# Selective attention with a SwiGLU block: earlier k and q copies, weight differences in eight pieces, and a subtraction and two stores at the end on GpSimd

## The chip, the cores and the metric

The kernel runs on one core of a Trainium2 chip. A core has TensorE (PE: matmuls, with weight loads, PEld, beside them), VectorE (DVE), ScalarE (ACT), GpSimd (POOL) and SyncE (SP), which here only issues transfers. The metric is the device time of one execution in microseconds (us). The span, which the profile shows, is the time from the first to the last instruction; it is some 1.8 us shorter than the metric in the kernel before.

## The reference, cut to what matters

```python
def _attn_ref(q, k, v, s):                 # 8 batches, 8 heads, 576 positions, 64 wide
    scores = scale * np.matmul(q, k.transpose(0, 1, 3, 2))
    bias = -(cum[:, :, :, None] - cum[:, :, None, :])      # cum: running sum of max(s, 0)
    scores = np.where(causal, -1000000000.0, scores + np.minimum(bias, 0.0))
    ...                                    # softmax
    return np.matmul(attn, v)

def _moe_ref(x, w_gate, w_val, w_out):     # 4608 tokens, 512 wide, 1536 inside
    g = x @ w_gate
    silu = g * (1.0 / (1.0 + np.exp(-g)))
    return silu * (x @ w_val) @ w_out
```

The attention of all heads, laid side by side, is the block's input x.

## The kernel before

TensorE gets one stream of matmuls in which attention (64 heads in 16 groups of four) and the block's nine tiles of 512 tokens are interleaved. The parts that matter:

From group 5 on, k and q reach their place as transposes by DMA (tiles pk, pq); VectorE then copies them to where the score matmuls read them. The copies wait in a list, from which each item of the block takes one or none:

```python
def split(hb, name, r):
    nc.vector.tensor_copy(KQ[hb % 2][r][64 * r : 64 * r + 64, kq, 0 : NR * S],
                          prs[name, hb][64 * r : 64 * r + 64, :])
...
first = 2 if late else 1                     # late: group 5
if step in (first, first + 1) and ci == 1:   # step: the head within the group before
    for r in range(NR):
        later.append((split, hb, "kq"[step - first], r))
```

From the third tile on the last product is done with seven block products in place of eight, for which sums and differences of the output weights are needed. VectorE makes the four differences in the third tile, in place:

```python
W_DIFFS = [(j, i) for i in (3, 4) for j in range(2)]
...
if todo and (i >= 24 if tt < FIRST7 else i % 4 == 2):
    weight_op(*todo.pop(0))
```

In the very last tile (`end`), the first of two groups of 128 rows ends with a subtraction and two stores, on GpSimd in other tiles, on VectorE and SyncE here. The second group, `ending`, follows on VectorE with three stores on SyncE:

```python
(nc.vector if end else nc.gpsimd).tensor_sub(y[:, 0:4:3, :], y[:, 0:4:3, :], y[:, 1:3, :])
flush()
def store(eng=nc.sync if end else nc.gpsimd):
    for i in range(2):
        eng.dma_start(out[a + i * HT : a + i * HT + 128, :], y[:, 2 * i : 2 * i + 2, :]...)
```

The softmax here doesn't subtract the row's maximum and nothing guards it: scores larger than these inputs give would overflow.

Of the kernel before, what the change touches and what calls it, by code (L numbers as in the profile page):

```python
# [19 lines left out]
def kernel(  # L20
# [11 lines left out]
    nc = tc.nc  # L32
# [47 lines left out]
    NPE = 5  # L80
# [23 lines left out]
    first = first_sbuf.enter_context(tc.tile_pool(name="first", bufs=1))  # L104
# [4 lines left out]
    with tc.manual_schedule():  # L109
# [35 lines left out]
        def view(b, w):  # L145
            return bank[b][:, 0:w]
# [15 lines left out]
        def load_qk(hb):  # L162
            load_one(hb, "k")
            load_one(hb, "q")

        def load_v(b, cs):
            if 0 in cs:
                loaded["v", b] = raw.tile([128, NCH, H, D], FP32, tag="rawv", bufs=1, name="rawv")
            t = loaded["v", b]
            for c in cs:  # L170
                n = 128 if c < 4 else TAIL
                nc.sync.dma_start(
                    t[0:n, c, :, :],
                    v[b, :, c * 128 : c * 128 + n, :].rearrange("h p d -> p h d"),
                )

        def cast_v(b, c, eng):
            n = 128 if c < 4 else TAIL
            dst, src_t = VT[b % 2][0:n, c, :, 0:D], loaded["v", b][0:n, c, :, :]
            if eng is nc.scalar:  # L180
                nc.scalar.copy(dst, src_t)
            else:
                eng.tensor_copy(dst, src_t)
# [8 lines left out]
        def aug(hb, engs):  # L192
            for hh in range(HB):
                r, e = divmod(hh, 2)
                r0 = 64 * (1 - r)
                bh = hb * HB + hh
                engs[hh].dma_start(  # L197
                    KQ[hb % 2][r][r0 : r0 + 4, :, e * S : (e + 1) * S],
                    HL[bh : bh + 1, :, :, :],
                )  # L200
# [48 lines left out]
        def cast_one(hb, name, eng):  # L249
            cts[name, hb] = cp.tile([128, J, NR, D], BF16, tag="c" + name, bufs=2, name="c" + name)  # L250
            dst = cts[name, hb].rearrange("x j r d -> x r j d")
            src_t = loaded[name, hb]
            if eng is nc.scalar:
                nc.scalar.copy(dst, src_t)
            else:
                eng.tensor_copy(dst, src_t)
# [11 lines left out]
        def scratch(hb):  # L268
            for name, SC in (("k", KS), ("q", QS)):
                nc.sync.dma_start(  # L270
                    SC[hb].rearrange("(x j) c -> x (j c)", j=J),
                    cts[name, hb].rearrange("x j r d -> x (j r d)"),
                )
# [3 lines left out]
        def transposes(hb):  # L277
            for name, SC in (("k", KS), ("q", QS)):
                prs[name, hb] = cp.tile([128, NR * S], BF16, tag="p" + name, bufs=1, name="p" + name)
                nc.sync.dma_start_transpose(prs[name, hb], SC[hb])  # L280
# [194 lines left out]
        def do_later(n):  # L475
            while n > 0 and later:
                f, *args = later.pop(0)
                f(*args)
                n -= 1

        def side(h, step, ci):
            bh = HB * h + step
            if bh == H + 3 and ci == 1:
                for c in range(5):
                    cast_v(1, c, nc.gpsimd)
            if h >= 3 and h + 3 < NHB and (step, ci) == (0, 1):
                load_qk(h + 3)
            hb = h + 1
            if NPE <= hb < NHB:
                late = hb == NPE  # L490
                if (step, ci) == (0, 1):
                    if late:
                        transposes(hb)
                    aug(hb, GP4)
                first = 2 if late else 1
                if step in (first, first + 1) and ci == 1:
                    for r in range(NR):
                        later.append((split, hb, "kq"[step - first], r))
            hb = h + 2
            if NPE <= hb < NHB:  # L500
                late = hb == NPE
                if (step, ci) == ((1, 1) if late else (0, 2)):
                    cast_one(hb, "k", nc.scalar)
                if (step, ci) == ((2, 1) if late else (1, 2)):
                    cast_one(hb, "q", nc.scalar)
                if (step, ci) == ((3, 1) if late else (2, 0)):
                    scratch(hb)
                if (step, ci) == (3, 3 if hb == NPE + 1 else 0) and not late:
                    do_later(NR * 2)
                    transposes(hb)  # L510
            if ci != 1:
                return
            bn = h // 2 + 1
            if 2 <= bn < B:
                if h % 2 == 0:
                    if step == 2:
                        load_v(bn, (0, 1))
                    if step == 3:
                        load_v(bn, (2, 3, 4))
# [65 lines left out]
        FIRST7 = 2  # L585
# [9 lines left out]
        def wo_parts(j):  # L595
            w = WO[j].rearrange("p (a h) (d n) -> p a h d n", h=2, d=2)
            return w, WS[:, j * (WKO // 2) : (j + 1) * (WKO // 2), :, :]

        def weight_op(j, i):
            w, t = wo_parts(j)  # L600
            if i == 0:
                nc.vector.tensor_add(t[:, :, 0, :], w[:, :, 0, 0, :], w[:, :, 1, 1, :])
            elif i == 1:
                nc.vector.tensor_add(t[:, :, 1, :], w[:, :, 0, 0, :], w[:, :, 0, 1, :])
            elif i == 2:
                nc.vector.scalar_tensor_tensor(
                    t[:, :, 2, :], in0=w[:, :, 1, 0, :], scalar=-1.0,
                    in1=w[:, :, 1, 1, :], op0=ALU.mult, op1=ALU.subtract,
                )
            elif i == 3:  # L610
                nc.vector.tensor_sub(
                    w[:, :, 0, 1, :], w[:, :, 0, 1, :], w[:, :, 1, 1, :]
                )
            else:
                nc.vector.tensor_sub(
                    w[:, :, 1, 0, :], w[:, :, 1, 0, :], w[:, :, 0, 0, :]
                )
# [71 lines left out]
        def down_seven(tt, hps, sus):  # L689
            W = [wo_parts(p // (WKO // 2))[0][:, p % (WKO // 2)] for p in range(NP)]  # L690
            end = tt == NTT - 1
# [49 lines left out]
            def m7(g):  # L741
                product(half(g, "1", "6")[0], False, True,
                        lambda p: hps[p][:, 2, cols[g]], lambda p: WS[:, p, 2, :])
# [22 lines left out]
            def seventh(g):  # L766
                a = tt * TT + g * 128
                y = Y[g]
                m7(g)
                nc.vector.tensor_add(  # L770
                    y[:, 0:4:3, :], DE[g],
                    view(B[g]["1"], DM).rearrange("p (a n) -> p a n", a=2),
                )
                give_banks(g, "1", "6")
                (nc.vector if end else nc.gpsimd).tensor_sub(  # L775
                    y[:, 0:4:3, :], y[:, 0:4:3, :], y[:, 1:3, :]
                )
                flush()

                def store(eng=nc.sync if end else nc.gpsimd):  # L780
                    for i in range(2):
                        eng.dma_start(
                            out[a + i * HT : a + i * HT + 128, :],
                            y[:, 2 * i : 2 * i + 2, :].rearrange("p a n -> p (a n)"),
                        )

                stores.append(store)
                if end:
                    flush()
                yield 0.757  # L790
# [149 lines left out]
                    state["pos"] = 1e9  # L940

        W_SUMS = [(j, i) for i in range(3) for j in range(2)]
        W_DIFFS = [(j, i) for i in (3, 4) for j in range(2)]
        LAGS = [0, 1.65] + [3.6] * NTT
        hook = {
            1: [lambda: prep_one(2, 0)],
# [5 lines left out]
        for tt in range(NTT):  # L952
            lo = H * (tt + 1) + LAGS[tt]
            hi = min(H * (tt + 2) + LAGS[tt + 1], BH + 2)
            span = 36 if tt < FIRST7 else 34.5
            if hi == BH + 2:
                span = 30
            n0 = 6 if tt == 0 else 0
            n = 0
            todo = {FIRST7 - 1: W_SUMS, FIRST7: W_DIFFS}.get(tt, [])  # L960
            for i, cost in enumerate(ffn_items(tt)):
                n += cost
                if todo and (i >= 24 if tt < FIRST7 else i % 4 == 2):
                    weight_op(*todo.pop(0))
                if i >= 2 * NFT or i % 4 == 1:
                    do_later(1)
                for f in hook.pop(n, ()):
                    f()
                pump(lo + (hi - lo) * min(1.0, max(0, n - n0) / (span - n0)))
# [31 lines left out]
```

## Time and profile before

| | before |
|---|---|
| time, median of the first 3 executions | 383.06 us (382.67 to 383.71) |
| span of the profiled execution, clock | 381.3 us, 1.000 |
| TensorE busy | 363.5 us, 95% |
| VectorE busy | 289.6 us, 76% |
| start of the last weight load | 376.26 us |
| last landing of a store | 380.41 us |

TensorE is the bound, so the time is read from where its stream stops, and from what comes after its end. Its busy time alone does not tell that, as ends of matmuls are modelled; start-to-start times do. The lines behind this are shown in the prediction.

### The profile page before, as it was taken

What the parts mean: (1) busy time and instruction counts of PE and PEld (TensorE: products, weight loads), DVE (VectorE), ACT (ScalarE), POOL (GpSimd) and SP (SyncE); (2) the same over time, 40 slices, a digit from 0 to 9 for tenths busy, and PEclk for the clock granted to TensorE, in tenths of its full rate; (3) what the DMA queues carried; (4) which work ended last, traced back from release to release, by engine and by line L of the source; (5) the groups of instructions that cost most, each with busy time, mean ns of one, the idle gap of its engine ahead of it and who ended that gap; (6) DMA issues with size and microseconds to landing.
All of it is one profiled execution on the core that took longest, in us unless ns stands there. A gap on an engine that the chain in (4) does not pass through costs nothing. (4 is left out here: it accounts for less than half of the span.)

```text
span 381.3 us, 8674 instructions
## 1 busy us (share of the span) xinstructions
PE 363.5 (95%) x3246; PEld 230.5 (60%) x3246; DVE 289.6 (76%) x577; ACT 242.7 (64%) x459; POOL 205.9 (54%) x326
## 2 busy tenths in 40 slices
PE   3779999998999999999999999999999999999995
PEld 3666556655555555865586558655875575476464
DVE  8666787456895799868986899589958866975983
ACT  8586788676977786578767876697455523323321
POOL 6684357545364636595458647775665426315220
PEclk9999999999999999999999999999999999999999
DMA  7999999997477998498739965987223213002003
GB/s 234 197 253 263 198 242 268 348 259 162 163 167 246 236 285 220 105 287 216 194 114 285 270 149 158 252 179 166 37 80 101 32 19 127 0 2 97 14 2 110
DMA packets 100729, 64.22 MB, mean 168 GB/s; under 512 B 81888, under 2 KB 85824, under 8 KB 100688
## 3 DMA queue, kind: packets, MB, share of 16 engines
q1 hardware_dynamic: 91248, 46.15, 48.6%
q0 software_dynamic: 9440, 17.53, 17.7%
q8 instruction: 25, 0.41, 0.4%
q14 instruction: 16, 0.13, 0.1%
HBM read 37.90 MB, written 19.86 MB: 151 GB/s over the span
## 5 line engine op out<-in xcount | busy, mean ns | idle before, releaser
L388 ACT ACTIVATE pt<-bank 128x512 bf16<-128x512 f32 x224 | 106.7, 506 | 26.5 <-PE bank L375 18.3
L626 PE MATMUL bank<-XT,wg 128*128 128x512 bf16 x432 | 110.9, 379 | 0.6 <-DVE pp L633 0.2
L641 PE MATMUL bank<-XT,wv 128*128 128x512 bf16 x432 | 110.8, 379 | 0.2
L631 ACT ACTIVATE th<-bank 128x512 bf16<-128x512 f32 x108 | 64.7, 599 | 60.0 <-PE bank L626 54.7
L633 DVE SCALAR_TENSOR_TENSOR pp<-th,bank 128x512 bf16<-128x512 bf16 x108 | 73.9, 684 | 30.2 <-ACT th L631 29.5
L649 DVE SCALAR_TENSOR_TENSOR ht<-pp,bank 128x512 bf16<-128x512 bf16 x108 | 74.1, 686 | 10.3 <-POOL ht L658 0.5
L658 POOL TENSOR_TENSOR ht<-ht 128x512 bf16<-128x512 bf16 x35 | 40.4, 1154 | 53.9 <-DVE su L656 53.8
L375 PE MATMUL bank<-kq 128*128 128x128 bf16 (+4 forms) x504 | 67.5, 240 | 1.6 <-DVE kq L284 1.1
L375 PEld LDWEIGHTS <-kq 128*128 128x128 bf16 x576 | 46.7, 99 | 34.8 <-issue 5.7
L641 PEld LDWEIGHTS <-wv 128*128 128x128 bf16 x432 | 38.6, 98 | 35.8 <-issue 0.4
L626 PEld LDWEIGHTS <-wg 128*128 128x128 bf16 x432 | 38.5, 98 | 35.2 <-issue 1.2
L391 POOL TENSOR_SCALAR_AFFINE_SELECT pt<-pt 128x512 bf16<-128x512 bf16 x64 | 41.8, 653 | 28.5 <-ACT pt L388 28.1
L413 PEld LDWEIGHTS <-pt 128*128 128x128 bf16 x960 | 41.1, 98 | 16.0
L413 PE MATMUL bank<-vt,pt 128*128 128x65 bf16 x840 | 41.8, 194 | 0.0
L447 POOL DMA_DIRECT2D xs<-ot x24 | 21.9, 912 | 31.7 <-DVE ot L430 31.7
L711 PEld LDWEIGHTS <-ht 128*128 128x128 bf16 x336 | 31.2, 98 | 4.3
L197 POOL DMA_DIRECT2D kq<-HL x52 | 31.2, 602 | 0.1
L430 DVE TENSOR_TENSOR ot<-bank,rc 128x320 bf16<-128x320 f32 x56 | 27.5, 492 | 1.9
L396 POOL TENSOR_SCALAR_AFFINE_SELECT pt<-pt 128x64 bf16<-128x64 bf16 x64 | 16.7, 261 | 18.9 <-ACT pt L388 18.7
L711 PEld LDWEIGHTS <-su 128*128 128x128 bf16 x252 | 23.6, 98 | 3.3
L670 PE MATMUL bank<-wo,ht 128*128 128x512 bf16 x96 | 24.6, 379 | 0.0
L775 POOL TENSOR_TENSOR ysb<-ysb 128x512 f32<-128x512 f32 x12 | 15.2, 1271 | 15.3 <-DVE ysb L770 15.3
(96 smaller groups left out, 396.9 us busy)
## 6 DMA issues: line engine op xcount, KB each, us to landing
rawk<-in_k_dram SPq DMA_DIRECT2D x15, 576.0 KB
rawq<-in_q_dram SPq DMA_DIRECT2D x15, 576.0 KB
rawv<-in_v_dram SPq DMA_DIRECT2D x32, 256.0 KB
out_dram<-ysb POOLq DMA_DIRECT2D x32, 256.0 KB, 3.8
xs<-ot POOLq DMA_DIRECT2D x24, 160.0 KB, 3.7
ks<-ck SPq DMA_DIRECT2D x11, 288.0 KB
qs<-cq SPq DMA_DIRECT2D x11, 288.0 KB
wg<-in_moe_w_gate_dram POOLq DMA_DIRECT2D x2, 768.0 KB, 12.6
```

Source lines behind the costliest of these rows:

```text
L197: engs[hh].dma_start(KQ[hb % 2][r][r0 : r0 + 4, :, e * S : (e + 1) * S], HL[bh : bh + 1, :, :, :],)
L375: nc.tensor.matmul(sc[:, o : o + w], T[:, 1, e * S + 128 * tj : e * S + 128 * (tj + 1)], T[:, 0, e * S + lo : e * S + hi], start=True, sto ...
L388: nc.scalar.activation(pt[:, c0 : c0 + W], sc[:, 0:W], AF.Exp, scale=0.125)
L391: nc.gpsimd.affine_select(pt[:, 1088:1600], pt[:, 1088:1600], pattern=[[0, 4], [1, 128]], compare_op=ALU.is_ge, fill=zreg, base=0, channel ...
L413: nc.tensor.matmul(av[:, bi * (D + 1) : (bi + 1) * (D + 1)], pt[:, c0 : c0 + 128], VT[b % 2][:, tj, h, :], start=(tj == 0), stop=(tj == bi),)
L626: nc.tensor.matmul(pg, WG[j][:, c, f0 : f0 + 128], xt[:, c, :], start=(c == 0), stop=(c == 3),)
L631: nc.scalar.activation(th, pg, AF.Tanh, scale=0.5)
L633: nc.vector.scalar_tensor_tensor(pp, in0=th, scalar=1.0, in1=pg, op0=ALU.add, op1=ALU.mult)
L641: nc.tensor.matmul(pv, WV[j][:, c, f0 : f0 + 128], xt[:, c, :], start=(c == 0), stop=(c == 3),)
L649: nc.vector.scalar_tensor_tensor(hp[:, 2 * k2 : 2 * k2 + 2, :].rearrange("p a n -> p (a n)"), in0=pp, scalar=0.5, in1=pv, op0=ALU.mult, op ...
L658: (nc.vector if ft == NFT - 1 else nc.gpsimd).tensor_sub(hp[:, 1:3, :], hp[:, 1:4:2, :], hp[:, 0:3:2, :])
L711: nc.tensor.matmul(ps, lhs(p), rhs(p), start=(first and p == 0), stop=(last and p == NP - 1), skip_group_check=True,)
```

## The change

Its intent: copies listed one or two heads sooner should be done before TensorE asks for them; differences in pieces of two thirds and one third should block VectorE for a shorter time each; and one VectorE instruction and two SyncE issues fewer in the tail should let the last stores go out sooner.

```diff
-                first = 2 if late else 1
+                first = 1 if hb < NPE + 2 else 0
...
-        def weight_op(j, i):
+        def weight_op(j, i, ps=None):
             w, t = wo_parts(j)
+            if ps is not None:
+                w, t = w[:, ps[0] : ps[1]], t[:, ps[0] : ps[1]]
...
-                (nc.vector if end else nc.gpsimd).tensor_sub(
+                nc.gpsimd.tensor_sub(
...
-                def store(eng=nc.sync if end else nc.gpsimd):
+                def store(eng=nc.gpsimd):
...
-        W_DIFFS = [(j, i) for i in (3, 4) for j in range(2)]
+        W_DIFFS = [(j, i, ps) for j in range(2) for ps in ((0, 2), (2, 3)) for i in (3, 4)]
...
-                if todo and (i >= 24 if tt < FIRST7 else i % 4 == 2):
+                if todo and (i >= 24 if tt < FIRST7 else i >= 2 and i % 2 == 0):
```

Two lines are added, so L775 of before is L777 after, L782 is L784, L801 is L803.

## The prediction

> **What bounds the kernel now.** I read the page's first two parts first.
>
> ```profile
> PE 363.5 (95%) x3246; PEld 230.5 (60%) x3246; DVE 289.6 (76%) x577; ACT 242.7 (64%) x459; POOL 205.9 (54%) x326
> PE   3779999998999999999999999999999999999995
> DVE  8666787456895799868986899589958866975983
> ```
>
> TensorE (PE) is nearly full from the fifth slice on. A busy PE need not be at its pace, so I took start-to-start times of its matmuls from the trace: a 128x512 matmul is followed after 215 to 216 ns (median 216, widest 221 where matmuls of one line follow one another), a 128x256 one after 109. Against 512/2.4 = 213 ns this is full speed. The excess over that pace is about 0.24 us in an ordinary 10 us, which is just the 2 to 3 ns per matmul. So PE sets the time, its instruction order is identical in both kernels (comparing the built orders shows no difference on PE), and the change can only take away or add PE stalls, or move the tail behind the last matmul. The start (up to 45 us, several us of stalls) is not touched.
>
> The stalls after 80 us, each over 0.2 us, are few: 1.26 us at 89.1; 0.24, 0.51 and 0.27 us at 143.95, 144.86 and 147.96; 0.23 and 0.23 us at 184.0 and 187.5; some 0.1 us in each of the slices around 226 and 266. Together about 2.9 us. That is all there is to win on PE.
>
> The first, in the timeline (start us, us, engine, line, work, idle before and its releaser):
>
> ```profile
> 87.66 0.46 DVE L284 COPY kq<-pk 64x1152 bf16<-64x1152 bf16 x1
> 88.71 0.69 DVE L633 SCALAR_TENSOR_TENSOR pp<-th,bank 128x512 bf16<-128x512 bf16 x1 [0.59 <-ACT th L631]
> 89.43 0.46 DVE L284 COPY kq<-pk 64x1152 bf16<-64x1152 bf16 x1
> 89.92 0.94 DVE L284 COPY kq<-pq 64x1152 bf16<-64x1152 bf16 x2
> 90.42 0.40 PE L375 MATMUL bank<-kq 128*128 128x128 bf16 x4 [1.10 <-DVE kq L284]
> ```
>
> PE sits waiting for scores of the first head of group 5 until the first copy of q is done (89.92 + 0.45 = 90.37; PE at 90.42).
>
> The stalls at 144 and 148 are VectorE being behind with freeing banks:
>
> ```profile
> 142.53 0.91 DVE L284 COPY kq<-pq 64x1152 bf16<-64x1152 bf16 x2
> 143.47 0.69 DVE L633 SCALAR_TENSOR_TENSOR pp<-th,bank 128x512 bf16<-128x512 bf16 x1
> 143.86 0.65 POOL L391 TENSOR_SCALAR_AFFINE_SELECT pt<-pt 128x512 bf16<-128x512 bf16 x1
> 144.08 0.85 DVE L615 TENSOR_TENSOR wo<-wo 128x768 bf16<-128x768 bf16 x1
> 144.85 0.68 DVE L649 SCALAR_TENSOR_TENSOR ht<-pp,bank 128x512 bf16<-128x512 bf16 x1
> 145.58 0.38 PE L375 MATMUL bank<-kq 128*128 128x128 bf16 x4 [0.34 <-DVE ht L649]
> ```
>
> PE takes the bank at 145.58, 0.05 us after L649 has read it out. From 132.2 to 148.2 DVE has no marked idle time: here it is the second bound. At 184 the pattern is the same, with the copies at 181.47, 182.60 and 183.05 in the way.
>
> The tail:
>
> ```profile
> 374.76 0.69 DVE L770 TENSOR_TENSOR ysb<-de,bank 128x512 f32<-128x512 f32 x1 [2.25 <-PE bank L711]
> 375.56 0.69 DVE L775 TENSOR_TENSOR ysb<-ysb 128x512 f32<-128x512 f32 x1
> 376.16 0.42 DVE L798 TENSOR_TENSOR de<-de,bank 128x256 f32<-128x256 f32 x1
> 376.27 0.81 SPq L782 DMA_DIRECT2D out_dram<-ysb  x2
> 376.50 0.42 DVE L801 TENSOR_TENSOR de<-de,ysb 128x256 f32<-128x256 f32 x1
> 376.83 0.42 DVE L805 TENSOR_TENSOR ysb<-de,ysb 128x256 f32<-128x256 f32 x1
> 377.17 0.41 DVE L810 TENSOR_TENSOR ysb<-de,bank 128x256 f32<-128x256 f32 x1
> 378.19 0.40 SPq L811 DMA_DIRECT2D out_dram<-ysb  x1
> ```
>
> The last store lands at 380.41 by the trace's landings, 2.2 us after its issue; the closing barrier takes the rest to 381.3.
>
> **What the Trainium skill says.** "TensorE: Matmul & The Clock Gate", Wait — 56ns, not 53.3ns?: warm matmuls start N/2.4 GHz plus about 2.5 ns apart, 215.7 ns at N=512. The trace agrees (215 to 216). "SBUF — State Buffer", Who interferes with whom: a DVE instruction with two SBUF inputs contends with a GpSimd instruction that reads SBUF, and the one that starts second waits. The trace agrees: the difference at 144.08 took 0.847 us, 0.427 of them beside L391 on GpSimd, while undisturbed ones took 0.550 and 0.553. "DMA: Bandwidth & Descriptors", Latency and other measured facts: first byte some 0.6 us for a DMA issued on SyncE and some 1 us for one from GpSimd. In the trace the last store pairs on GpSimd landed 2.33, 2.65, 2.90 and 3.14 us after their issue began, those on SyncE 2.04 to 2.36.
>
> **The change part by part.**
>
> *k and q copies.* I mapped the new DVE order on the times of before. Group 5: the first k copy moves to about 77.6 (DVE is idle from there to 79.67; its transpose landed at 78.68, so it ends by 79.2), the second to 83.4 (0.41 us idle there), the first q copy to 87.7. It is done at 88.1, before PE asks at 89.16, and the next banks have over 2.9 us of slack. So the whole stall goes, less a little that comes back at 97.6, where a bank has only 0.21 us: -1.2 us. Group 10: the first k copy moves from 176.5 to 172.1, where DVE idles 0.25 and soon 0.62 us; its transpose landed at 166.8. The second k copy takes its place, so one copy of 0.46 fewer lies directly before 183.5, and both stalls of 0.23 fit in it: -0.45 us. The same for groups 12 and 14: -0.2 us. Odd groups 9 to 15 have no stalls to lose, and landings lie 4 us and more ahead.
>
> *Group 8 and the weight differences*, in the stretch 132.2 to 148.2. Four copies before, four after. Of the differences three lay inside (1.65 us undisturbed, at 0.55). After, the pieces are 128x512 (as L656: 0.434 us) and 128x256 (as L657: 0.284). Two large ones come before 132.2; two large and four small lie inside: 2 x 0.434 + 4 x 0.284 = 2.00 us, 0.35 more. And the first k copy is moved to about 132.2, but its transpose, issued at 124.47 behind loads of v and stores, landed only at 133.00. DVE takes instructions in order, so it would stand 0.7 us, less the 0.25 it idles there anyway. Walking on from there with the measured durations, DVE is 0.9 to 1.2 us late at 137 to 142, where banks have 0.30 (137.97) and 0.05 us (142.67) of slack, then catches up, as only one copy and a small piece stand before L633 and L649 at 143.5 to 145. I get 1.5 us of PE stalls in place of 1.0. Without the wait for the landing I get about 0.9. Weighted: +0.25 us.
>
> *Tail.* One DVE instruction of 0.69 leaves. On GpSimd it takes 1.27 (all twelve: 1.257 to 1.283), starting 0.13 us after L770 as elsewhere: 375.58 to 376.84. The two stores then issue at 376.8 and 377.35 and land 2.33 and 2.65 later: 380.0, against 380.41. On DVE L798 moves up to 375.4, but L801 and L805 have two SBUF inputs, and GpSimd's subtraction reads SBUF: L801 would stand until 376.84, so L805 runs 377.2 to 377.6 and the last SyncE store issues at 378.1. That is 0.1 us gained, not the 0.7 that an instruction less suggests: -0.1 us.
>
> Sum: -1.2 - 0.45 - 0.2 + 0.25 - 0.1 = -1.7 us; 383.06 - 1.7 = 381.4.
>
> **Rivals.** (1) Head-of-line: copies listed sooner wait for transposes. Group 8 is the case, groups 5 and 7 are near it (group 7's landed at 110.09, new place about 110.8). For: from 120 to 140 us the stretches of 10 us show a DMA share of 1.01 and 1.15, the fullest but for 40 to 50 and 160 to 170. Against: everything before it, loads and scratch writes, also moves up with PE. At worst 1.5 us more of stalls: 382.9, no gain. (2) The pieces do what they are for: no wait at 132, fewer of them collide with GpSimd, the 1.0 us at 144 to 148 goes as well. Against: total work of DVE there grows. Then 380.2. (3) The stores from GpSimd end the kernel: their landing at 3.1 us, as for the third and fourth of a row, or descriptors held up by DVE, would give 377.35 + 3.14 = 380.5, 0.1 us longer than now instead of 0.1 shorter: 381.6. (4) The subtraction does not collide and both queues share the stores: SyncE's last issue at 377.4, 0.35 us better: 381.1.
>
> **Range and chances.** No part can reach 2% (7.7 us): the PE stalls that the change can touch are 2.9 us, the tail moves by tenths, and losing would need several waits of 2 us each. Range 380.5 to 382.6. Faster by over 2%: 0.01; within: 0.98; slower: 0.01.
>
> **What would show it.** Right: PE goes straight from L413 to L375 near 88 us; no wait of PE for L284; no PE gap near 183 and 186; a k copy near 131 that starts at its transpose's landing, with DVE idle before it put down to a DMA, and PE stalls near 136 and 141; L801 lasting or starting late beside L775 on GpSimd. Wrong: PE gaps at 140 to 147 gone or doubled, or the last landing being GpSimd's and later than 3.9 us behind the last matmul's start (376.37 before, landing 380.41). The prediction fails as a whole if the span drops by under 0.5 or over 2.6 us.

## The result, and the profile after

The changed kernel is **slower**: 385.56 us median (383.69 to 386.00, 6 runs) against 383.00 (382.60 to 383.71, 6 runs). The ratio is 1.006, 95% interval 1.0038 to 1.0082. (A ratio here is the mean time of one kernel's fast runs over that of the other's of the same rounds, so it is not quite the ratio of the medians.) It is within 2%, but outside my range and on the other side of zero.

The profiled execution was the fastest of the seven: 383.69 us, span 381.5. The others had spans of 383.1 to 383.9. So I look for causes in the trace and take sizes from the timed runs.

Page of the changed kernel, its first two parts:

```profile
PE 360.0 (94%) x3207; PEld 229.2 (60%) x3246; DVE 290.5 (76%) x580; ACT 242.3 (64%) x459; POOL 209.2 (55%) x329
PE   3789999999999999999999999999999999999992
DVE  7776776467893999678977997699768858957963
```

The last digit of PE fell from 5 to 2: TensorE ends earlier. Its busy time can't be compared, as 39 matmul records are missing (3207, not 3246). All 3246 weight loads are there, in the same order, so I compare their starts. The last one starts at 376.26 us before and at 373.77 after: **TensorE's stream is 2.49 us shorter, and the kernel is not.** The closing stretch, from that start to the span's end, grew from 381.33 - 376.26 = 5.07 us to 381.53 - 373.77 = 7.76.

First the stream. Timeline of the changed kernel at group 5's first head:

```profile
86.75 0.57 DVE L284 COPY kq<-pq 64x1152 bf16<-64x1152 bf16 x1
87.99 0.43 PE L413 MATMUL bank<-vt,pt 128*128 128x65 bf16 x9
88.26 0.39 PE L375 MATMUL bank<-kq 128*128 128x128 bf16 x4
```

The copy of q is done at 87.32, PE goes from L413 to L375 without a wait. The stall of 1.26 us is gone. The third tile:

```profile
129.85 0.92 POOL L447 DMA_DIRECT2D xs<-ot  x1 [0.83 <-DVE ot L430]
130.06 0.96 DVE L284 COPY kq<-pk 64x1152 bf16<-64x1152 bf16 x1
136.15 0.46 PE L413 MATMUL bank<-vt,pt 128*128 128x65 bf16 x10 [0.18 <-DVE ot L430]
141.25 0.34 PE L413 MATMUL bank<-vt,pt 128*128 128x65 bf16 x6 [0.34 <-DVE ot L430]
146.33 1.02 PE L643 MATMUL bank<-XT,wv 128*128 128x512 bf16 x4 [0.33 <-DVE ot L430]
```

The first two lines are GpSimd's issue of a transfer and, beside it, group 8's first copy, which took 0.96 us, not some 0.46. The stalls have other places and causes, and add up to a little more than before. Now the tail:

```profile
372.28 0.69 DVE L772 TENSOR_TENSOR ysb<-de,bank 128x512 f32<-128x512 f32 x1 [2.25 <-PE bank L713]
373.10 1.27 POOL L777 TENSOR_TENSOR ysb<-ysb 128x512 f32<-128x512 f32 x1 [8.47 <-DVE ysb L772]
373.33 1.33 DVE L803 TENSOR_TENSOR de<-de,ysb 128x256 f32<-128x256 f32 x1
374.58 0.41 DVE L807 TENSOR_TENSOR ysb<-de,ysb 128x256 f32<-128x256 f32 x1
374.67 1.09 POOL L784 DMA_DIRECT2D out_dram<-ysb  x2 [0.30 <-POOL ysb L777]
375.44 0.39 SPq L813 DMA_DIRECT2D out_dram<-ysb  x1
```

L803 took 1.33 us instead of 0.42: it stood until GpSimd's subtraction was through at 374.37, the contention that the prediction counted with. The last landing is at 378.83, 1.58 us sooner than before. Yet the span ends at 381.53. (Counted from the last weight load's start, so without TensorE's gain, the last landing is 5.06 us behind, 4.16 before: it comes 0.90 us later. GpSimd's second store landed 3.44 us after its issue began, and SyncE's last 3.39, before 2.22.) What lies between shows only in the view of the closing line's own instructions (engine, operation, count; nanoseconds least, median, longest; first and last start in us). Before:

```profile
L996 SPq EVENT_SEMAPHORE  x11: 17/28/28, 378.6 to 381.3; - x11
L996 POOLq DRAIN  x3: 46/102/5190, 365.9 to 381.1; - x3
```

After:

```profile
L998 SPq EVENT_SEMAPHORE  x11: 17/28/2612, 375.9 to 381.5; - x11
L998 POOLq DRAIN  x3: 46/102/5662, 375.1 to 381.3; - x3
```

GpSimd's queue ends with a DRAIN. Before, it starts at 365.94 and takes 5.190 us, so it is over at 371.13, 4.01 us after GpSimd's last instruction (L658, to 367.12) and 9.3 us before the last store lands: nobody notices. After, it ends at 375.09 + 5.66 = 380.75, which is 4.99 us after the issue of its last store (375.76) and 1.92 us after the last landing. The closing exchange of all engines, 0.75 to 0.8 us, starts only then. The 2612 ns of SyncE are its wait for the landing of GpSimd's second store, at 378.66; SyncE's last wait for a landing was over at 378.99.

### The profile page after: what moved, and what is told of

It is laid out like the page before. It is cut to its first block, busy times and chain, and to the rows that moved or that the text cites. A ratio compares the mean times of both kernels' runs of the same rounds, so it can differ in the third digit from the quotient of the medians.

```text
span 381.5 us, 8639 instructions
## 1 busy us (share of the span) xinstructions
PE 360.0 (94%) x3207; PEld 229.2 (60%) x3246; DVE 290.5 (76%) x580; ACT 242.3 (64%) x459; POOL 209.2 (55%) x329
## 4 chain that ended last, share of the span: by engine, by line
PE 79%; SPq 7%; DVE 4%; ACT 2%; DMA 2%; issue 1%; POOL 1%; POOLq 0%; DVEq 0%
PE bank L643 20%; PE bank L628 20%; PE bank L713 16%; PE bank L375 8%; SPq L172 7%; PE bank L413 6%; PE bank L672 5%; DMA rawq<-in_q_dram 2%; ACT pt L388 2%; PE wide L375 2%; DVE ht L651 1%; DVE pp L635 1%; PE one L311 1%; DVE ot L430 1%; DVE kq L284 0%
## 5 line engine op out<-in xcount | busy, mean ns | idle before, releaser
L628 PE MATMUL bank<-XT,wg 128*128 128x512 bf16 x420 | 109.8, 379 | 1.1 <-DVE pp L635 0.2
L643 PE MATMUL bank<-XT,wv 128*128 128x512 bf16 x411 | 109.3, 379 | 1.4 <-DVE ot L430 0.3
L375 PE MATMUL bank<-kq 128*128 128x128 bf16 (+4 forms) x504 | 67.5, 240 | 0.3 <-DVE ht L651 0.2
L375 PEld LDWEIGHTS <-kq 128*128 128x128 bf16 x576 | 46.5, 99 | 32.5 <-issue 5.1
L413 PEld LDWEIGHTS <-pt 128*128 128x128 bf16 x960 | 41.1, 98 | 16.8 <-issue 0.9
L413 PE MATMUL bank<-vt,pt 128*128 128x65 bf16 x840 | 41.8, 194 | 0.5 <-DVE ot L430 0.5
L447 POOL DMA_DIRECT2D xs<-ot x24 | 21.7, 906 | 27.5 <-DVE ot L430 27.5
L777 POOL TENSOR_TENSOR ysb<-ysb 128x512 f32<-128x512 f32 x13 | 16.5, 1271 | 23.8 <-DVE ysb L772 23.8
L396 POOL TENSOR_SCALAR_AFFINE_SELECT pt<-pt 128x64 bf16<-128x64 bf16 x64 | 17.5, 274 | 18.5 <-ACT pt L388 18.3
```

Of the source, the lines that this page charges most:

```text
L375: nc.tensor.matmul(sc[:, o : o + w], T[:, 1, e * S + 128 * tj : e * S + 128 * (tj + 1)], T[:, 0, e * S + lo : e * S + hi], start=True, sto ...
L413: nc.tensor.matmul(av[:, bi * (D + 1) : (bi + 1) * (D + 1)], pt[:, c0 : c0 + 128], VT[b % 2][:, tj, h, :], start=(tj == 0), stop=(tj == bi),)
L628: nc.tensor.matmul(pg, WG[j][:, c, f0 : f0 + 128], xt[:, c, :], start=(c == 0), stop=(c == 3),)
L643: nc.tensor.matmul(pv, WV[j][:, c, f0 : f0 + 128], xt[:, c, :], start=(c == 0), stop=(c == 3),)
```

## The experiments

Twelve kernels, in three jobs; in each job they share the runs of the kernel before (11 of them: medians 382.81, 383.12 and 382.81 us). All gave correct results.

| kernel | median us | ratio to before, 95% interval | closing stretch us | end of GpSimd's DRAIN after its last instruction | last landing / DRAIN's end us |
|---|---|---|---|---|---|
| before | 383.06 | | 5.07 | 4.01 | 380.41 / 371.13 |
| change | 385.56 | 1.0060 (1.0038, 1.0082) | 7.76 | 4.99 | 378.83 / 380.75 |
| no_tail | 382.26 | 0.9987 (0.9962, 1.0011) | 5.08 | 4.01 | 380.06 / 370.77 |
| tail_only | 386.30 | 1.0090 (1.0074, 1.0105) | 7.74 | 4.96 | 380.65 / 382.55 |
| kq_only | 381.14 | 0.9967 (0.9932, 1.0001) | 5.07 | 4.01 | 379.08 / 369.80 |
| pieces_only | 383.36 | 1.0008 (0.9989, 1.0026) | 5.09 | 4.01 | 381.41 / 372.12 |
| sub_pool | 383.21 | 0.9993 (0.9967, 1.0019) | 5.68 | 4.01 | 379.92 / 379.77 |
| store_pool | 384.77 | 1.0052 (1.0019, 1.0086) | 7.09 | 4.91 | 379.93 / 381.81 |
| probe_small | 383.64 | 1.0015 (0.9992, 1.0037) | 6.37 | 4.01 | 379.30 / 380.73 |
| better | 380.09 | 0.9923 (0.9902, 0.9944) | 4.93 | 4.01 | 379.20 / 370.06 |
| no_tail_again | 382.28 | 0.9981 (0.9965, 0.9997) | 5.08 | 4.01 | 378.83 / 369.55 |
| g5_after | 381.89 | 0.9989 (0.9963, 1.0014) | 5.09 | 4.01 | 377.94 / 368.63 |
| g8_late | 381.44 | 0.9964 (0.9950, 0.9977) | 5.08 | 4.01 | 379.30 / 370.01 |
| diffs_ahead | 380.94 | 0.9945 (0.9928, 0.9963) | 5.09 | 4.01 | 378.12 / 368.82 |

The second table is how TensorE's stream moved against the trace of before: the difference of the starts of the same weight load, taken over stretches (minus is time won, us). Up to 77 us the program is the same in all of them, and its difference is what the first transfers happen to do.

| trace | to 77 us | near 80 | near 90 | 134 to 150 | 184 to 188 | later | sum from 77 us on |
|---|---|---|---|---|---|---|---|
| change | -0.91 | 0.00 | -1.27 | +0.24 | -0.34 | -0.21 | -1.58 |
| no_tail | +0.78 | +0.45 | -1.27 | +0.24 | -0.34 | -0.22 | -1.13 |
| no_tail_again | -0.71 | 0.00 | -1.27 | +0.96 | -0.35 | -0.22 | -0.87 |
| kq_only | -0.28 | +0.51 | -1.27 | +0.38 | -0.46 | -0.21 | -1.05 |
| pieces_only | +1.05 | 0.00 | 0.00 | +0.29 | -0.36 | +0.01 | -0.06 |
| tail_only | -0.65 | 0.00 | 0.00 | 0.00 | 0.00 | 0.00 | -0.01 |
| sub_pool | -0.76 | +1.26 | -1.27 | +0.23 | -0.34 | -0.21 | -0.33 |
| store_pool | +0.47 | +0.39 | -1.27 | +0.23 | -0.35 | -0.22 | -1.21 |
| probe_small | -0.28 | 0.00 | -1.27 | +0.97 | -0.33 | -0.21 | -0.84 |
| g5_after | -0.89 | 0.00 | -1.27 | +0.23 | -0.35 | -0.21 | -1.59 |
| g8_late | -0.37 | +0.77 | -1.27 | +0.31 | -0.34 | -0.22 | -0.75 |
| diffs_ahead | -0.56 | 0.00 | -1.27 | +0.19 | -0.46 | -0.21 | -1.75 |
| better | +1.93 | 0.00 | -1.27 | -1.07 | -0.46 | -0.21 | -3.00 |

The first column, from -0.91 to +1.93, is as large as the differences between single executions of one kernel here (some 2 us), so the second table settles more than the times do.

My theory after the result (theory 1 in the expectations): GpSimd's closing DRAIN ends a fixed time after GpSimd's last instruction and holds the end. Rivals: the copies or pieces lose in the executions without a kept trace (2); the landings of GpSimd's stores are what costs (3); the subtraction blocking VectorE costs (4).

### no_tail: the change without its third part

```diff
-                nc.gpsimd.tensor_sub(
+                (nc.vector if end else nc.gpsimd).tensor_sub(
-                def store(eng=nc.gpsimd):
+                def store(eng=nc.sync if end else nc.gpsimd):
```

> The change without its third part: k, q copies sooner and eight pieces, but the last groups' subtraction on VectorE and its stores on SyncE as before. Theory 1 (GpSimd's closing DRAIN, which begins to count only after its last instruction, holds up the end): the 2 us or so that TensorE gains reach the end, 380.5 to 381.5 us, 4 to 5 us under the change; GpSimd's DRAIN ends by about 369 to 371 us and does not touch the end. Rival 2 (the loss is from the copies or the pieces in the unprofiled executions, seen in their lower mean clock): stays at 384 to 386 us. Rival 3 (the stores' landing is late, not the DRAIN): faster too, but then the change's last landing of 378.8 us leaves little to win: 382 to 383 us.

Measured: 382.26 us, 3.3 us under the change's median (2.8 us by the ratios to before, as the two were not run side by side). The closing stretch is 5.08 us as before. So rival 2 falls. But the gain over before is only 0.13%, and 382.26 lies above what I expected (380.5 to 381.5), in the range I had given to rival 3. This run alone doesn't tell the DRAIN from the landings, and it opens a second question: where TensorE's gain stays.

### tail_only: only the third part

The edit is the third part of the diff above, on the kernel before.

> Only the third part: the last group's subtraction and stores on GpSimd. Theory 1: TensorE as before, and the end held by GpSimd's DRAIN 5 us or more after its last store's issue: 385 to 388 us, slower than before by 2 to 5 us, with the mean clock down as TensorE idles at the end. Rival 2: 383.0 us, unchanged. Rival 3 (landings): 383 to 384 us.

Measured: 386.30 us, ratio 1.009. TensorE's stream is that of before to 0.01 us in all stretches after 77 us, and the closing stretch is 7.74 us, so +2.67 us are made in the tail alone. The DRAIN's line:

```profile
L996 POOLq DRAIN  x3: 46/102/5639, 376.9 to 383.1; - x3
```

It ends at 382.55, the last landing is at 380.65. Times less spans are 2.2 us here and with the change, 1.8 before; what lies in these 0.35 us outside the span I have not found. The time is 0.9% longer, 2.8 to 4.0 us by its interval; 2.67 and 0.35 together lie in it.

### sub_pool: the subtraction on GpSimd, the stores on SyncE

On no_tail, only `nc.gpsimd.tensor_sub(` is kept from the third part.

> The change with the last group's stores back on SyncE, the subtraction left on GpSimd. In the traces so far GpSimd's closing DRAIN ended 4.0 us after its last compute instruction (before, no_tail) and 5.0 us after its last store's issue (the change, tail_only). Theory 1: the subtraction ends some 2.1 us after L772 begins and the DRAIN 4.0 us later, so the end comes 0.2 to 0.6 us after no_tail's: 382.4 to 383.0 us, and the DRAIN is what the closing waits for. Rival 3 (it is the stores from GpSimd and their landings that cost, the DRAIN only shadows them): the same as no_tail, 382.2 us, with the DRAIN over before the last landing. VectorE's L803 waits for the subtraction either way.

Measured: 383.21 us, 0.2 above the range of theory 1; closing stretch 5.68, 0.60 more than no_tail. The DRAIN ends 4.01 us after the subtraction, at 379.77, but the last store lands at 379.92: here the landing is last by 0.15 us, not the DRAIN, against what I wrote. It is late as VectorE's L803 stood for the subtraction (1.324 us). So in this kernel rival 4 sets the end, by a little. In the change it does not: there the last landing is 1.92 us before the DRAIN's end.

### store_pool: the subtraction on VectorE, the stores on GpSimd

On no_tail, only `def store(eng=nc.gpsimd):` is kept.

> The change with the last group's subtraction back on VectorE, its two stores left on GpSimd. Theory 1: the stores' issue ends near 2.7 us after L772 begins and the DRAIN 5.0 us later: 1.5 to 2 us or more above no_tail, 384 to 385 us, about 1 us under the change. Rival 3 (landing decides): at most 0.5 us above no_tail, 382.3 to 382.8. Rival 4 (it is the subtraction on GpSimd that blocks VectorE, and with it all the rest): like no_tail, 382.3.

Measured: 384.77 us; closing stretch 7.09, 2.01 more than no_tail, though VectorE isn't blocked (L803 0.418 us) and the last landing is at 379.93. The DRAIN ends 4.91 us after the last issue, at 381.81. Rivals 3 and 4 fall as main causes. (The last landing did come later, 4.42 us after the last weight load's start in place of 4.16, but 1.88 us before the DRAIN's end.)

### probe_small: one tiny instruction for GpSimd at the end

```diff
                 nc.sync.dma_start(out[a : a + 128, H0], y[:, 0, :])
+                last = small.tile([128, 8], FP32, tag="last", name="last")
+                nc.gpsimd.tensor_copy(last, y[:, 0, 0:8])
```

> no_tail with one more instruction: GpSimd copies 128x8 numbers of the last group's finished output into a tile that nobody reads. It moves no data that matters, issues no DMA and lies behind VectorE's last instruction. Theory 1: the DRAIN ends 4.0 us after it, near 3.5 us after VectorE's last end, so the span grows by 1.2 to 1.8 us against no_tail: 383.5 to 384.1 us. Rival 3 (only DMAs from GpSimd do it): no change, 382.2 us.

Measured: 383.64 us, within the range of theory 1; but its interval takes in 1, and 0.97 us were lost in its third tile, so the time alone settles nothing and the trace has to. Timeline and the DRAIN of this kernel:

```profile
376.53 0.19 POOL L815 COPY last<-ysb 128x8 f32<-128x8 f32 x1 [10.52 <-DVE ysb L812]
```

```profile
L1000 POOLq DRAIN  x3: 46/102/4223, 376.5 to 381.2; - x3
```

An instruction of 0.19 us whose result nobody reads makes the closing stretch 1.29 us longer. Its end, 376.72, plus 4.01 is 380.73, when the DRAIN is over; the last landing was at 379.30. **This shows theory 1 by itself: no store, no blocked engine, only a late last instruction of GpSimd.** In 11 traces GpSimd's last instruction computes, and the DRAIN ends 4.01 us after it; in the other three it issues a store, and the DRAIN ends 4.91 to 4.99 us after that. Why it takes that long, no run shows.

### kq_only and pieces_only: the first two parts alone

Each is its part of the diff, on the kernel before.

> Only the copies of k and q listed sooner. By the shifts in the two traces (1.28 us at 90.4 us, 0.2 to 0.3 at 184, 0.2 at 227) 381.0 to 381.6 us if the part is a gain by itself; if the wait of group 8's first copy for its transpose cost anything, stalls at 138 to 143 us of up to 0.8 us appear here too.

> Only the eight pieces. If the pieces do what they are for, the stalls at 144 to 148 us (1.0 us before) shrink and the time falls by up to 1 us, 382.0 to 382.9; if, as in my prediction, VectorE has more work in all there and it merely shifts, the stalls stay at 0.8 to 1.3 us and the time at 383.0 within 0.3.

Measured: kq_only 381.14 us, within the range, though its interval reaches 1.0001, with one execution of 385.32. The second table has its stream: 1.27 us at 90, 0.46 at 184 and 0.21 later are won; 0.51 near 80 and 0.38 in the third tile are lost. pieces_only 383.36 us, ratio 1.0008: nothing won. The third tile is 0.29 us worse; 0.36 come back at 184, where the trace of before had two small stalls. This part moves no copy, so the copies cannot be what won it. What differs in the traces is a wait of VectorE for GpSimd (L658) just ahead of these stalls, which is there in before and tail_only and not in pieces_only; why the pieces take it away is not shown. Before:

```profile
180.75 0.69 DVE L649 SCALAR_TENSOR_TENSOR ht<-pp,bank 128x512 bf16<-128x512 bf16 x1 [0.49 <-POOL ht L658]
```

The loss near 80 us is rival (1) of my prediction at a place that I had called near it. Timeline of kq_only:

```profile
79.82 0.45 DVE L284 COPY kq<-pk 64x1152 bf16<-64x1152 bf16 x1 [2.49 <-DMA pk<-ks]
80.20 0.44 DVE L470 COPY XT<-bank 128x576 bf16<-128x576 bf16 x1
80.69 0.38 PE L626 MATMUL bank<-XT,wg 128*128 128x512 bf16 x1 [0.35 <-DVE XT L470]
```

Group 5's first copy stands for its transpose (landed at 79.80 here), the copy of XT stands behind it, and the second tile's gate needs XT. In the trace of before the transpose landed at 78.68, in time.

### no_tail_again, g5_after, g8_late, diffs_ahead: where TensorE's gain stays

no_tail_again is no_tail as a control. The other three are no_tail with one edit each:

```diff
# g5_after: group 5's list later and in the order of need
-                if step in (first, first + 1) and ci == 1:
-                    for r in range(NR):
-                        later.append((split, hb, "kq"[step - first], r))
+                if step in (first, first + 1) and ci == (3 if late and step == first else 1):
+                    for i in range(NR):
+                        nm, r = ("kq"[i], step - first) if late else ("kq"[step - first], i)
+                        later.append((split, hb, nm, r))
# g8_late: group 8 as in the kernel before
-                first = 1 if hb < NPE + 2 else 0
+                first = 1 if hb in (NPE, NPE + 1, NPE + 3) else 0
# diffs_ahead: whole differences, ahead of the third tile's first gate; W_DIFFS as before (cut here)
...
+            if tt == FIRST7:
+                for d in W_DIFFS:
+                    weight_op(*d)
```

> no_tail once more, as the control of the three kernels beside it. In its trace TensorE stood 0.45 us at 81 us, 1.35 us between 137 and 149 us. 382.3 us. If the gain over before that its trace shows (some 1.1 us of TensorE stalls less) is real, 381.7 to 382.3; single executions of 384 to 385, as there was one in each of no_tail and kq_only, would mean that a copy listed sooner sometimes waits long for a late transpose.

> no_tail with group 5's first copy behind VectorE's copy of XT, and those of the first pair before the second pair's. If the copy that waited for its transpose's landing held up the copy of XT, and with it the second tile's first gate, TensorE's stall of 0.45 us near 81 us goes and the time falls by 0.4 us against no_tail, to 381.9; slow single executions go as well, if they came from that wait. If the stall at 81 is from elsewhere, no change.

> no_tail with group 8's copies listed where the kernel before has them. My prediction's third step: the first copy waiting for its transpose's landing, beside pieces that are more work in all, makes VectorE late at 137 to 143 us. If the early copy is the cause, the stalls of 1.35 us between 137 and 149 us fall to 1.0 us or less, all behind 143 us, and the time by 0.2 to 0.5 us. If the pieces are the cause, the stalls stay at 1.2 to 1.4 us as in pieces_only.

> no_tail with the four differences whole again, and ahead of the third tile's first gate, where VectorE idles 3.9 us. If the stalls between 137 and 149 us come from too much VectorE work in that stretch, in whatever pieces, 2.2 us of it less takes them all away, 1.0 to 1.3 us: 381.0 to 381.3. If they came from the early copy's wait for its transpose, some 0.3 to 0.7 us stay.

Measured: 382.28, 381.89, 381.44 and 380.94 us. Their intervals overlap for all but diffs_ahead against the control; the traces say more.

The control had no stall near 80 us this time, but lost 0.96 us in the third tile, not 0.24:

```profile
131.47 0.47 DVE L284 COPY kq<-pk 64x1152 bf16<-64x1152 bf16 x1 [1.13 <-DMA pk<-ks]
135.83 1.02 PE L628 MATMUL bank<-XT,wg 128*128 128x512 bf16 x4 [0.53 <-DVE ht L651]
```

Group 8's first copy stood 1.13 us for its transpose, and four microseconds later a bank was not free. In the trace of the change the same copy found its transpose landed. So each copy listed sooner is a race with a transfer that some executions lose: near 80 us the nine traces with group 5's copy at the early place show 0, 0.45, 0, 0.51, 1.26, 0.39, 0, 0.77 and 0 us, on average 0.38. With g5_after (and in better, below) VectorE's copy of XT comes first, and the stall is 0.00 in both traces; two traces are too few to exclude it, but the order excludes this way to it. Its slow executions, 383.45 and 384.06, did not go away, so those are from something else. The start, with its spread, and group 8's copy are candidates; no trace of one was kept.

In the third tile, g8_late left the loss at +0.31, and diffs_ahead at +0.19, but at other places: g8_late's stalls lie from 141 us on (0.24 to 0.61 us each), diffs_ahead's all before 138:

```profile
132.00 0.45 DVE L284 COPY kq<-pk 64x1152 bf16<-64x1152 bf16 x1 [1.86 <-DMA pk<-ks]
135.94 1.02 PE L628 MATMUL bank<-XT,wg 128*128 128x512 bf16 x4 [0.27 <-DVE ht L651]
137.43 0.46 PE L413 MATMUL bank<-vt,pt 128*128 128x65 bf16 x10 [0.47 <-DVE ot L430]
```

So both causes are there: the early copy's wait, and the differences' work in a stretch that VectorE can't take. Each remedy alone left the loss of the other. Against my expectations, neither edit alone brought this stretch back to the level of before in its trace. diffs_ahead's time is nevertheless the best of the three; its other executions have no kept trace, so how much of that is the third tile, and how much group 5's copy being in time (0.00 near 80 us, where g8_late lost 0.77), stays open.

### better: both remedies and the old tail

It joins g5_after, g8_late and diffs_ahead on the kernel before, and gives one of SyncE's last stores to ScalarE's queue:

```diff
-                nc.sync.dma_start(out[a : a + 128, HD:DM], y[:, 1, :])
...
                 nc.scalar.copy(y[:, 2, :], p21)
+                nc.scalar.dma_start(out[a : a + 128, HD:DM], y[:, 1, :])
```

> A version of mine: tail on VectorE as before, with one of SyncE's stores given to ScalarE's queue; copies sooner, but group 5's first only after the copy of XT (it held up TensorE 0.5 us in no_tail and kq_only) and those that TensorE needs first before the others, group 8's as before; the four weight differences whole and ahead of the third tile's first gate, where VectorE idles, in place of eight pieces. Expected against before: 1.26 us of group 5's stall, the 1.0 us of stalls at 144 to 148 us, 0.4 at 184 and 187, 0.2 later, and 0.5 at the end: 379.5 us (379.0 to 381.0), below every kernel so far. If TensorE's stalls only shift, 381.

Measured: 380.09 us, ratio 0.9923 (0.9902 to 0.9944): **2.9 us under the mean of before, and it beats both kernels.** In the profiled execution, its slowest (381.94 us), the start cost 1.93 us, and from 77 us on the stream is 3.00 us shorter. The trace shows where the start was lost: at 24 us TensorE was 2.94 us ahead of before; then it stood 3.28 us, as VectorE's cast of v (L183) waited for its load, and from 26.20 to 29.62 its granted clock was 0.5. No other kept trace has a lowered clock between 17 us and the end of TensorE's stream. The third tile has no stall of over 0.2 us left. VectorE makes the differences where it waited for TensorE anyway:

```profile
123.94 0.56 DVE L612 TENSOR_TENSOR wo<-wo 128x768 bf16<-128x768 bf16 x1 [1.17 <-PE bank L671]
124.42 1.02 DVE L616 TENSOR_TENSOR wo<-wo 128x768 bf16<-128x768 bf16 x2
125.92 0.69 DVE L634 SCALAR_TENSOR_TENSOR pp<-th,bank 128x512 bf16<-128x512 bf16 x1 [0.48 <-ACT th L632]
```

After the differences it still waits 0.48 us. The store on ScalarE's queue brought 0.14 us (closing stretch 4.93, not 5.07) of the 0.5 that I expected: the last issue came sooner, but the last store landed 2.56 us after it, not 2.22.

## Why the prediction was right or wrong

**Wrong: the tail.** The step that failed is "The last store lands at 380.41 by the trace's landings, 2.2 us after its issue; the closing barrier takes the rest to 381.3", from which "That is 0.1 us gained". I took the last landing as what the closing waits for. It waits for GpSimd's DRAIN too, which in the kernel before had been over for 9.3 us. I moved GpSimd's last instruction from 367.1 to the very end without asking what follows it there. In place of -0.1 us the term is +2.7 us in the closing stretch (tail_only, 7.74 against 5.07), and 0.9% (3.4 us) in time. The landings were mis-sized too: I had them 2.33 and 2.65 us after GpSimd's issues and 2.2 after SyncE's last, and so the last one 0.4 us sooner than before (380.0 against 380.41). In the change they took 2.59, 3.44 and 3.39 us, and counted from the last weight load the last one came 0.90 us later. By my estimate from these numbers, that alone would have made the tail 0.9 us longer without any DRAIN. The line that would have told it was in the profile of before: a DRAIN of 5190 ns. As probe_small has it, 4.01 us after 376.84 (my own end of the subtraction) is later than 380.41 already, and the stores come on top.

**Right, in the tail:** that L801 would stand beside the subtraction (1.327 us, until it was through), that the stores issue in a row behind it, and that little is gained for VectorE. Rival (3) had the right engine, GpSimd, and a part of the loss, the late landing, but not what the end waited for, and with +0.1 us not the size.

**Right: group 5**, -1.2 predicted, -1.27 in all eleven traces that have the copies sooner. **Near in size, the cause in part not shown: later groups**, -0.45 and -0.2 predicted, -0.34 and -0.21 measured in the change. The -0.21 is the copies' (pieces_only has +0.01 there). The -0.34 at 184 is not shown to be: pieces_only, with all copies where they were, has -0.36. The prediction's "At 184 the pattern is the same" had overlooked VectorE's wait of 0.49 us for GpSimd at 180.75.

**Right in part, group 8 and the pieces.** +0.25 predicted; +0.24 in the trace of the change. That near-equality is luck: the wait for the landing, which I put at 0.45 us on balance, was not there in that trace, but the copy ran beside GpSimd's issue of a transfer (L447) and took 0.96 us. My two branches were -0.1 us without the wait and +0.5 with it. Five traces in which the copy waited 0.4 us or less show +0.23 to +0.24, two in which it waited 0.71 and 1.13 us show +0.97 and +0.96: a late landing costs, as predicted, but both branches were too low. The seven traces with both parts as in the change show +0.23 to +0.97, on average 0.44.

**Under-weighted: head of line at group 5.** I saw the landing at 78.68 and wrote that the copy "ends by 79.2". It does in some executions. In others the stall near 80 us takes 0.4 to 1.3 us back. With the averages above the first two parts bring -1.27 + 0.38 + 0.44 - 0.35 - 0.21 = -1.0 us on TensorE, where I had -1.6; the times of no_tail and no_tail_again, 0.13% and 0.19% under before (0.5 and 0.7 us, their intervals 0.6 to 0.9 us either way), agree with that.

Together: 0.9984 (the mean of these two) times 1.009 (tail_only) is 1.0074, and the change measured 1.006 (1.0038 to 1.0082). The parts account for the whole. (The mean clock of 0.984 to 0.994 in the change's other executions is no mark of a loss by itself: the two fastest of no_tail_again, 381.41 and 381.58 us, have 0.993.) What stays open is why the DRAIN takes as long as it does, the 0.35 us between time and span, and why the start of this kernel differs by up to 2.8 us from one execution to another. A remark of rival (1) was wrong as well: the stretches from 20 to 50 and others reach a DMA share of 1.12 to 1.21 too, so 120 to 140 us is not exceptional.

## What to carry to other kernels

Before you give work at the end of a kernel to an idle engine, look at what that engine's queue does after its last instruction: here GpSimd had been idle for 10.5 us and still set the end when it was used once more, for 0.2 us. Cutting instructions into pieces did not help VectorE in a stretch with too much work for it (pieces_only, 1.0008); moving the work to where it waits did, together with the later copy (better). An operation listed sooner in an in-order queue must be sure of its data in every execution, as a late transfer holds up what is queued behind it.

## What the Trainium skill lacked or had wrong

- GpSimd's closing DRAIN: "VectorE: DVE Perf Modes", The DRAIN you can't avoid, knows two kinds, the flush after each VectorE operation and the runtime's own of about 12 ns, constant, on all five engines. Those on the closing line of this kernel's program have that size on SyncE alone (7 to 13 ns in the trace of before); the longest is 402 ns on ScalarE, 574 on VectorE, 2155 on TensorE and 5190 on GpSimd. Whether the page means these is not shown. On GpSimd it takes 4.2 to 5.7 us, and ends 4.01 us after the last compute instruction (11 traces) or 4.91 to 4.99 us after the issue of the last store (3 traces). I found no page that says what a late last instruction of GpSimd costs; here it was 1.29 us for a copy of 128x8 numbers and 2.67 us for the subtraction with two stores.
- "DMA: Bandwidth & Descriptors", Latency and other measured facts, gives the first byte as some 0.6 us for a transfer from SyncE and 1 us for one from GpSimd. It lacks that landings get later along a row of stores: 2.33, 2.65, 2.90 and 3.14 us after the start of their issue for four in a row in the trace of before, and 3.44 (GpSimd's second) and 3.39 us (SyncE's last) in the change, where both queues store at once.
